# Moving one quad of exponentials in the last chunk of an attention block to VectorE, and new order constants for a kernel that plans its own instruction order

## The chip, the cores and the metric

One core of one Trainium2 chip. The metric is the device time of the one launch in microseconds; before the change the median of three runs is 809.28 us (809.02 to 810.05). Five engines work side by side, each through its own list of instructions in order: TensorE (PE, matmuls), ScalarE (ACT), VectorE (DVE), GpSimd (POOL) and SyncE (SP, which here only issues DMAs). They wait for each other through semaphores.

## The reference

An adaLN-conditioned transformer block over S = 2048 tokens of D = 640, with 32 heads of 20 and an MLP width of F = 1536, in bfloat16:

```
sa, ca, ga, sb, cb, gb = split(silu(c) @ w_mod, 6)
h = layernorm(x) * (1 + ca) + sa
q, k, v = split(h @ wqkv)
o = softmax(q k^T / sqrt(20)) v          # 32 heads, 2048 x 2048 scores each
x = x + ga * (o @ wo)
h = layernorm(x) * (1 + cb) + sb
x = x + gb * (((h @ w_gate) * (h @ w_up)) @ w_down)
```

Most of the element-wise work is the exponential: 32 x 2048 x 2048 of them.

## The kernel before

**Tiling.** The queries come in five chunks of 512, 512, 512, 256 and 256 (`CHUNKS`). The 32 heads are eight sets of four heads, one head for each group of 32 rows of the PE array. A pair of chunk and head set is an item, 40 in all, numbered 0 to 39 (`items`, the text calls them sets too; set 38 is the seventh head set of the last chunk). The work of an item is cut in units of 128 x 512 scores: 64 units in an item of the first three chunks, 32 in one of the last two.

**Two ways for an exponential.** A unit goes one of two ways.

- On ACT: two units at a time make a score round (L1492, the matmul of K and Q into one of two PSUM sets) and one ACTIVATE with Exp over 128 x 1024 (L1530, here called an exp). The results lie in PP, two buffers of four slots, so that eight exps may be outstanding; the product with V (L2179, from PP) frees a slot.
- On VectorE, by a piecewise approximation, four units at a time, a quad: each unit's score is evicted with an add and a max into int16 (L1554, to DB); then one operation over the whole quad masks out the mantissa (L1586, to DSS), one the exponent (L1594, to DSS), and mantissa times value is multiplied either on VectorE in one piece (L1591) or on GpSimd in four (L1646). Two terms come out of a quad, so that it costs PE twice the products with V (L2179, from DSS).

`QUADS[chunk][head set]` says how many quads an item has. All other units are ACT's.

**The end of an item.** When all its products with V are done, VectorE transposes the accumulator (L1724) and takes the reciprocal of the row sums (L1728), GpSimd multiplies (L1730, to OTn; VectorE in the last item), VectorE transposes back (L1738, to OcT), and four or five DMAs on SP's queue (L1751) write the rows to Ocp. Products of the next item use the same accumulator bank and start only after L1724. The last item is not written to Ocp: its OcT is used directly.

**The rest.** When a chunk is through, its suffix follows: the out projection (wo), the second layernorm, gate and up projections (weights loaded to stg and stx), and the down projection (wd). The suffix of a chunk is spread between the scores of the next one (L951, four narrow matmuls side by side); that of the last chunk is a tail behind everything (L947, wide matmuls). The projections of q, k and v lie mostly under the first chunk.

**What sets the order.** Nothing is ordered at run time. When it is built, the kernel runs a list scheduler (`Sched`, `pick_pe`): each task has a planned duration, and the order in which the scheduler starts them is written out as each engine's instruction list, with semaphore waits for the dependencies. Choices on PE (which comes next: a score round, products with V, a projection, or a filler matmul L2546 that only keeps PE active) hang on constants, and these may be overridden for each item in the table `STAGE`, taken over when the item's products with V begin (L2188, `stage`). The constants:

- `EAGER`, `D_LATE`, `D_RES`, `DL`: when the scores of a quad are due, how far ahead they may ride along with a score round, how late they force a round of their own, and when a PSUM bank is held back for them
- `PVMIN`, `PVMAX`, `PVCAP`, `PVTOL`: how many products with V are gathered before they are issued, and how far a batch may run past the time at which the next score round is ready
- `HOLD`, `X_LATE`: how long PE is left waiting for a score round that is nearly ready, and when a projection matmul is split into two halves to fit in front of one
- `FILL_MIN`, `FILL_Z`, `Z_LATE`: below which recent activity fillers are issued
- `XBACK`, `XDPRIO`, `TPRIO`: whether a quad's multiply may go to VectorE and with which priority against its other work
- `STEAL_GAP`: when ACT takes over a PSUM eviction

```
def stage(it):
    globals().update(base)
    globals().update(STAGE.get(it, {}))
...
t.cond = lambda c0=c0, st_=st_: st_["xby"] is None and c0() and xjob[0] >= XBACK
```

Of the kernel before, what the change touches and what calls it, by code (L numbers as in the profile page):

```python
# [29 lines left out]
STEAL_GAP = 200  # L30
# [299 lines left out]
def emit_program(nc, sched, nsem_dma=56):  # L330
# [97 lines left out]
    with nc.Block() as block:  # L428
# [20 lines left out]
        def _(e):  # L449
# [22 lines left out]
EAGER = 7  # L472
# [43 lines left out]
FILL_MIN = 4190.746  # L516
FILL_HARD = 0.0
FILL_Z, Z_LATE = 3300.0, 0.0
# [29 lines left out]
    8: {"PVCAP": 15, "PVMAX": 3, "Z_LATE": 19.94, "FILL_Z": 3656.07, "FILL_MIN": 4663.83, "TPRIO": 0.57, "X_LATE": -175.04, "EAGER": 16, "PVMIN": 1, "XBACK": 3, "STEAL_GAP": 194.45},  # L548
    9: {"X_LATE": -14.35, "PVCAP": 12, "XBACK": 0, "HOLD": 65, "PVMIN": 3, "D_LATE": 24, "PVMAX": 6, "D_RES": 23, "FILL_MIN": 4552.44, "XDPRIO": 1.63},
    10: {"PVMAX": 8, "X_LATE": -27.967, "EAGER": 5, "D_LATE": 15, "PVCAP": 8, "XBACK": 0, "HOLD": 155, "FILL_Z": 3693.44, "Z_LATE": -95.95, "PVMIN": 5, "XDPRIO": 1.25, "PVTOL": 199, "D_RES": 17},  # L550
    11: {"DL": 0.443, "X_LATE": 54.31, "FILL_MIN": 4086.76, "PVTOL": 270, "PVMAX": 6, "PVCAP": 14, "XBACK": 2, "D_LATE": 22, "Z_LATE": -74.79, "EAGER": 4},
    12: {"DL": 0.459, "FILL_MIN": 5116.53, "D_LATE": 11, "STEAL_GAP": 194.93, "X_LATE": -138.337, "HOLD": 125, "FILL_Z": 3256.59, "PVMIN": 1, "D_RES": 29},
    13: {"DL": 0.417, "D_RES": 4, "HOLD": 99, "PVMAX": 4, "TPRIO": 0.51, "PVMIN": 5, "STEAL_GAP": 145.61, "PVCAP": 13, "FILL_MIN": 4574.64, "FILL_Z": 2424.75, "PVTOL": 324, "Z_LATE": 38.05},
    14: {"D_LATE": 14, "D_RES": 16, "FILL_MIN": 4279.59, "EAGER": 11, "X_LATE": -150.94, "STEAL_GAP": 200, "PVTOL": 374, "FILL_Z": 3396.29, "HOLD": 50, "XDPRIO": 1.59, "PVMAX": 10, "TPRIO": 1.17, "PVCAP": 9},
    15: {"X_LATE": -189.21, "EAGER": 15, "Z_LATE": -100, "D_RES": 5, "HOLD": 65, "PVMAX": 4, "PVMIN": 4, "PVTOL": 199, "STEAL_GAP": 191.33, "FILL_MIN": 4305.09},
    16: {"D_RES": 67, "HOLD": 88, "PVCAP": 11, "PVMIN": 3, "PVTOL": 299, "STEAL_GAP": 83.35, "EAGER": 7, "Z_LATE": 121.81, "FILL_MIN": 4640.79, "FILL_Z": 2909.17, "D_LATE": 20, "X_LATE": 34.41},
    17: {"D_LATE": 23, "PVMAX": 10, "PVMIN": 5, "FILL_MIN": 4666.58, "EAGER": 4, "FILL_Z": 3806.89, "PVCAP": 9, "XBACK": 4, "Z_LATE": 10.27},
    18: {"FILL_MIN": 5006.36, "D_RES": 10, "X_LATE": 88.33, "FILL_Z": 2885.8, "HOLD": 80, "Z_LATE": -17.94, "PVTOL": 99, "XBACK": 0, "STEAL_GAP": 258.74, "EAGER": 5},
    19: {"DL": 0.471, "D_LATE": 16, "FILL_MIN": 3976.707, "HOLD": 140, "TPRIO": 1.09, "PVCAP": 15, "X_LATE": 3.27, "PVMAX": 10, "FILL_Z": 3225.84},
    20: {"DL": 0.391, "D_LATE": 14, "PVCAP": 13, "FILL_MIN": 5232.96, "FILL_Z": 3888.52, "HOLD": 110, "STEAL_GAP": 143.97, "X_LATE": 36.5, "XBACK": 0, "PVTOL": 174, "Z_LATE": 264.18, "EAGER": 5, "D_RES": 38},  # L560
    21: {"D_RES": 10, "PVCAP": 20, "HOLD": 111, "PVMAX": 3, "PVMIN": 2, "D_LATE": 19, "X_LATE": 10.44, "STEAL_GAP": 193.54, "FILL_MIN": 4451.89, "FILL_Z": 2458.3, "XBACK": 0, "Z_LATE": 146.94, "EAGER": 6},
    22: {"PVMAX": 4, "FILL_MIN": 2993.41, "D_RES": 17, "EAGER": 6, "D_LATE": 14, "PVCAP": 10, "PVTOL": 224, "STEAL_GAP": 173.23},
    23: {"PVTOL": 197, "PVMAX": 8, "D_RES": 23, "Z_LATE": -56.49, "STEAL_GAP": 273.34, "FILL_MIN": 5236.36, "EAGER": 7, "HOLD": 185, "FILL_Z": 4231.28, "D_LATE": 14, "XDPRIO": 1.93, "TPRIO": 1.16},
    24: {"DL": 0.464, "PVCAP": 13, "PVMAX": 9, "PVMIN": 2, "FILL_MIN": 4034.81, "EAGER": 7, "STEAL_GAP": 200, "X_LATE": 41.65, "HOLD": 125, "XDPRIO": 0.3, "D_LATE": 14},
    25: {"DL": 0.549, "STEAL_GAP": 200, "HOLD": 129, "X_LATE": 20.01, "D_RES": 13, "FILL_MIN": 3705.17, "PVCAP": 13, "D_LATE": 18, "PVMIN": 5, "Z_LATE": 116.92, "PVMAX": 9, "XBACK": 1},
    26: {"DL": 0.411, "D_RES": 15, "X_LATE": -208.68, "PVMAX": 9, "PVCAP": 14, "STEAL_GAP": 200, "FILL_MIN": 3859.63, "XBACK": 3, "EAGER": 8},
    27: {"DL": 0.473, "D_LATE": 6, "PVMAX": 6, "EAGER": 2, "D_RES": 75, "PVTOL": 249, "PVMIN": 2, "X_LATE": -93.66, "FILL_MIN": 4986.69},
    28: {"PVCAP": 13, "X_LATE": 94.44, "D_RES": 23, "HOLD": 80},
    29: {"PVCAP": 14, "PVMAX": 7, "D_RES": 46, "FILL_MIN": 3820.529, "HOLD": 65, "PVTOL": 299, "X_LATE": 14.16, "Z_LATE": -100},
    30: {"X_LATE": 10.24, "PVCAP": 19, "FILL_MIN": 3782.61, "D_LATE": 16, "EAGER": 9, "PVMAX": 4, "STEAL_GAP": 217.05, "PVTOL": 224, "XDPRIO": 1.57, "PVMIN": 1},  # L570
    31: {"D_RES": 19, "FILL_MIN": 4905.173, "D_LATE": 13, "PVMIN": 2, "X_LATE": 36.868, "HOLD": 155, "PVTOL": 274, "PVCAP": 13},
# [2050 lines left out]
```

## Time and profile before

| | |
|---|---|
| median of 3 runs | 809.28 us (809.02 to 810.05) |
| the profiled execution's own time | 809.42 us |
| its span in the profile | 807.6 us |
| busy: PE, ACT, DVE, POOL | 793.6, 764.0, 691.6, 364.6 us |
| exps (L1530) on ACT | 808, 743.8 us busy |
| quads on VectorE | 108 |
| mean granted PE clock | 1.00 |

The profile is one execution on the chip. A group of instructions is given as line, engine, operation, output<-input with its shapes, and count; then busy microseconds, the mean of one in ns, the idle time of the engine in front of them and what ended most of it. Matmuls are pipelined, so that the busy time of PE holds part of its waiting. ACT's operations overlap too: the busy time of a group is the union of its instructions, not their sum. In a timeline row stand start, duration, engine, line, operation and count, in brackets the idle time before it and what released it. The chain is followed back from the last instruction through what released each step. "issue" is time in which an engine waited for nothing that the profile shows.

### The profile page before, as it was taken

To read this page: it belongs to the slowest core of one execution; us is meant where nothing else is said; L and a number is where in the kernel's file an instruction comes from. 1 tells how busy PE (TensorE), PEld (TensorE's weight loads), DVE (VectorE), ACT (ScalarE), POOL (GpSimd) and SP (SyncE) were. 2 spreads that over 40 slices of the span, in tenths; PEclk is the share of its full clock that TensorE was granted. 3 is DMA by queue.
4 is the path that set the end of the run, shared out by engine and by line. 5 is a ranking of instruction groups with operands and counts; after the bars stand their busy time and mean duration, and the time that the engine had idled before them with its cause. 6 is when DMAs were issued, how large, how long until landed. Compare 5 with 4: busy or idle time off the path is not lost.

```text
span 807.6 us, 29760 instructions
## 1 busy us (share of the span) xinstructions
PE 793.6 (98%) x12789; PEld 307.5 (38%) x12789; DVE 691.6 (86%) x1275; ACT 764.0 (95%) x854; POOL 364.6 (45%) x370
## 2 busy tenths in 40 slices
PE   9999999999999999999999999999999999999998
PEld 4433333222233222333233333333245543544577
DVE  7979987999999899998998999999598874778873
ACT  7899999999999999999999999999999999999922
POOL 3303266465665452444456244334267552652710
PEclk9999999999999999999999999999999999999999
DMA  9624211114230235100401221001203363005010
GB/s 313 208 82 109 68 46 41 43 38 126 86 72 23 58 86 142 30 13 22 95 6 31 54 51 33 4 24 53 59 6 71 81 144 71 13 23 128 8 37 18
DMA packets 108577, 52.80 MB, mean 65 GB/s; under 512 B 76043, under 2 KB 108447, under 8 KB 108447
## 3 DMA queue, kind: packets, MB, share of 16 engines
q1 hardware_dynamic: 107519, 49.75, 23.4%
q8 instruction: 102, 1.67, 0.8%
q10 hardware_dynamic: 928, 1.15, 0.4%
q14 instruction: 28, 0.23, 0.1%
HBM read 39.88 MB, written 8.41 MB: 60 GB/s over the span
## 4 chain that ended last, share of the span: by engine, by line
PE 51%; ACT 38%; issue 6%; DVE 4%; DMA 1%; SPq 0%; ACTq 0%; DVEq 0%
ACT PP L1530 38%; PE ps_all L1492 16%; PE ps_all L951 16%; PE ps_all L2179 11%; PE ps_all L947 3%; DVE DB L1554 1%; PE ps_all L1211 1%; PE ps_all L2546 1%; DMA wm<-in_w_mod_dram 1%; PE ps_all L1147 1%; PE ps_all L1914 1%; DVE DSS L1586 1%; PE ps_all L1108 1%; DVE DSS L1594 0%; SPq L1751 0%
## 5 line engine op out<-in xcount | busy, mean ns | idle before, releaser
L1530 ACT ACTIVATE PP<-ps_all 128x1024 bf16<-128x1024 f32 x808 | 743.8, 1130 | 5.0 <-PE ps_all L1492 2.6
L1646 POOL TENSOR_TENSOR DSS<-DB,DSS 128x512 bf16<-128x512 bf16 x264 | 299.8, 1157 | 321.1 <-DVE DSS L1594 276.1
L1554 DVE TENSOR_SCALAR DB<-ps_all 128x512 int16<-128x512 f32 x432 | 287.9, 683 | 52.6 <-PE ps_all L1492 50.5
L1492 PE MATMUL ps_all<-QT,KT 32*128 32x512 bf16 (+1 forms) x2560 | 315.4, 340 | 7.2 <-ACT PP L1530 3.8
L1492 PEld LDWEIGHTS ps_all<-QT,KT 32*128 32x128 bf16 x2560 | 82.2, 91 | 260.6 <-ACT PP L1530 223.2
L2179 PE MATMUL ps_all<-PP,Vf 128*32 128x512 bf16 (+1 forms) x2032 | 158.2, 343 | 0.0
L951 PE MATMUL ps_all<-h2T,stg 128*32 128x512 bf16 (+2 forms) x1948 | 119.5, 326 | 0.1
L2179 PE MATMUL ps_all<-DSS,Vf 128*32 128x512 bf16 (+2 forms) x1056 | 85.0, 343 | 0.3 <-DVE DSS L1594 0.2
L1594 DVE TENSOR_SCALAR DSS<-DB 128x2048 int16<-128x2048 int16 x108 | 76.9, 712 | 0.1
L1586 DVE TENSOR_SCALAR DSS<-DB 128x2048 int16<-128x2048 int16 x108 | 76.0, 703 | 0.5
L2179 PEld LDWEIGHTS ps_all<-PP,Vf 128*32 128x32 bf16 x2032 | 45.1, 94 | 78.7 <-issue 72.4
L1730 POOL TENSOR_TENSOR OTn<-OT,invT 128x512 bf16<-128x512 f32 (+1 forms) x39 | 38.1, 977 | 52.4 <-DVE invT L1728 52.2
L951 PE MATMUL ps_all<-wd,hprod 128*32 128x320 bf16 (+1 forms) x1300 | 61.1, 286 | 0.2 <-DVE DB L1554 0.2
L951 PEld LDWEIGHTS ps_all<-h2T,stg 128*32 128x32 bf16 x1948 | 42.3, 95 | 35.9 <-issue 24.4
L1591 DVE TENSOR_TENSOR DSS<-DB,DSS 128x2048 bf16<-128x2048 bf16 x42 | 52.3, 1249 | 0.1
L951 PEld LDWEIGHTS ps_all<-wd,hprod 128*32 128x32 bf16 x1300 | 28.5, 96 | 21.1 <-issue 13.3
L2179 PEld LDWEIGHTS ps_all<-DSS,Vf 128*32 128x32 bf16 (+1 forms) x1056 | 27.0, 95 | 18.5 <-issue 8.9
L951 PE MATMUL ps_all<-wV,hT 128*32 128x320 bf16 (+1 forms) x696 | 32.5, 290 | 0.0
L1211 PE MATMUL ps_all<-hT,wq 128*32 128x512 bf16 x375 | 31.2, 383 | 0.2
L951 PE MATMUL ps_all<-wo,Ocp 128*32 128x320 bf16 (+1 forms) x660 | 30.3, 281 | 0.2
L2546 PE MATMUL ps_all<-ident 128*32 128x512 bf16 x344 | 30.0, 383 | 0.0
L1724 DVE STREAM_TRANSPOSE OT<-ps_all 128x512 f32<-128x512 f32 (+1 forms) x40 | 24.1, 602 | 6.0 <-PE ps_all L2179 5.8
(130 smaller groups left out, 528.6 us busy)
## 6 DMA issues: line engine op xcount, KB each, us to landing
stg<-in_B_w_gate_dram SPq DMA_DIRECT2D x44, 160.0 KB
stg<-in_B_w_up_dram SPq DMA_DIRECT2D x44, 160.0 KB, 3.1
QT<-q_rows SPq DMA_DIRECT2D x22, 128.0 KB, 2.4
KT<-k_rows SPq DMA_DIRECT2D x84, 32.0 KB, 2.6
wm<-in_w_mod_dram SPq DMA_DIRECT2D x3, 800.0 KB
x<-in_A_x_dram SPq DMA_DIRECT2D x7, 320.0 KB
xck<-in_A_x_dram SPq DMA_DIRECT2D x3, 640.0 KB, 4.5
wd<-in_B_w_down_dram SPq DMA_DIRECT2D x1, 1920.0 KB
```

Source lines behind the costliest of these rows:

```text
L951: return lambda e, b: e.matmul(ps[32 * x:32 * x + 32, b, c0 + o:c0 + o + w], lhs()[:, 32 * x:32 * x + 32], rhs() if w == n else rhs()[:, o ...
L1211: f = [lambda e, b_, k=k, x=x: e.matmul(ps[x:x + min(32, w - x), b_, :], wx[:, k, r0 + x:r0 + min(x + 32, w)], hT[tc][:, k, :], tile_posit ...
L1492: ems.append(lambda e, i=i, kt=kt: e.matmul(dstf()[:, i * u.n:(i + 1) * u.n], KT[32 * u.s:32 * u.s + 32, u.j, kt * 128:(kt + 1) * 128], QT ...
L1530: return e.activation(PPs[g % 2][:, cellp["p"], 0:nu * 512], ps[:, b0:b0 + nu, :].rearrange("p b c -> p (b c)"), AFT.Exp, scale=ESCALE)
L1554: return e.tensor_scalar(DBl[st_["slot"]][:, x * 512:(x + 1) * 512], bank(cell["b"]), EBIAS, 0.0, op0=ALU.add, op1=ALU.max)
L1586: return e.tensor_scalar(DSl[st_["ss"][0]][:, :], DBl[st_["slot"]][:, :], 0x7F, 0x3F00, op0=ALU.bitwise_and, op1=ALU.bitwise_or)
L1591: return e.tensor_tensor(d, DBl[st_["slot"]][:, :].bitcast(BF16), d, ALU.mult)
L1594: return e.tensor_scalar(DSl[st_["ss"][1]][:, :], DBl[st_["slot"]][:, :], 0x7F80, 2, op0=ALU.bitwise_and, op1=ALU.bitwise_or)
L1646: return e.tensor_tensor(d, DBl[st_["slot"]][:, x * w:x * w + w].bitcast(BF16), d, ALU.mult)
L1730: f3 = lambda e: e.tensor_tensor(OTn[:, 0:n].rearrange("p (b c r) -> p b r c", c=32, r=2), OT[:, 0:n].rearrange("p (b r c) -> p b r c", c= ...
L2179: ems.append(lambda e, i=i, kt=kt, stt=stt, stp=stp: e.matmul(ps[32 * s:32 * s + mc, BPV, 0:u.n], Vf[:, (kt * H + 4 * u.j + s) * VW:(kt * ...
L2546: task.emits = [lambda e, x=x: e.matmul(ps[32 * x:32 * x + 32, b_, :].rearrange("p (a b) -> p a b", a=4), ident[:, 32 * x:32 * x + 32], id ...
```

## The change

Two tables of constants change and no code. In the last chunk the first and third head sets (sets 32 and 34) get one quad more and the seventh (set 38) one less, 109 quads for 108. In `STAGE`, of the 40 entries those of sets 0 to 7, 14, 20, 23 and 38 stay, and the other 28, from set 8 on, get other values; which tasks exist besides the moved units does not hang on them, only their order, their engine where two are possible, and where a matmul is halved. Its core:

```
          (3, 5, 2, 4, 3, 4, 4, 4),
          (4, 2, 4, 4, 4, 4, 4, 4),
          (1, 2, 1, 2, 2, 1, 1, 2),
-         (0, 2, 1, 1, 3, 0, 3, 2))
+         (1, 2, 2, 1, 3, 0, 2, 2))
...
-    8: {..., "TPRIO": 0.57, "X_LATE": -175.04, "EAGER": 16, ..., "STEAL_GAP": 194.45},
-    9: {..., "D_RES": 23, "FILL_MIN": 4552.44, "XDPRIO": 1.63},
-    10: {"PVMAX": 8, ..., "HOLD": 155, ..., "PVMIN": 5, "XDPRIO": 1.25, "PVTOL": 199, "D_RES": 17},
+    8: {..., "TPRIO": 0.57, "EAGER": 16, ..., "STEAL_GAP": 194.45, "XDPRIO": 2.05},
+    9: {..., "D_RES": 23, "FILL_MIN": 4103.55, "XDPRIO": 1.63, "PVTOL": 224},
+    10: {"PVMAX": 9, ..., "HOLD": 110, ..., "PVMIN": 2, "XDPRIO": 1.25, "PVTOL": 199, "D_RES": 17},
...
-    34: {"X_LATE": 150, "D_LATE": 22, "FILL_MIN": 3900.9, ..., "PVMAX": 9, ..., "XBACK": 2, "Z_LATE": 90.81},
-    35: {..., "FILL_MIN": 2500, "STEAL_GAP": 179.748, ..., "HOLD": 121, ..., "EAGER": 12, "XBACK": 3, "XDPRIO": 1.7, ...},
-    36: {"DL": 0.524, ..., "X_LATE": 67.38, ..., "PVCAP": 15, ...},
-    37: {"D_LATE": 12, ..., "PVCAP": 13, ..., "XBACK": 1, "XDPRIO": 1.88, "HOLD": 65, ..., "FILL_Z": 4023.76},
+    34: {"X_LATE": 150, "D_LATE": 24, "FILL_MIN": 4158.98, ..., "PVMAX": 11, ..., "XBACK": 0, "Z_LATE": 90.81, "HOLD": 80},
+    35: {..., "FILL_MIN": 2704.26, "STEAL_GAP": 209.68, ..., "HOLD": 106, ..., "XBACK": 4, "XDPRIO": 0.37, ..., "EAGER": 8},
+    36: {"DL": 0.524, ..., "X_LATE": 8.69, ..., "PVCAP": 18, ...},
+    37: {"D_LATE": 14, ..., "PVCAP": 15, ..., "XDPRIO": 1.88, "HOLD": 35, ..., "FILL_Z": 3731.25, "PVMAX": 6, "EAGER": 9},
     38: {"D_RES": 60, "PVMAX": 7, "PVTOL": 375, "D_LATE": 14, "EAGER": 5, "TPRIO": 0.3, "FILL_MIN": 3948.58, "XBACK": 3, "X_LATE": 4.46},
-    39: {"FILL_MIN": 3089.11, ..., "EAGER": 8, "HOLD": 140, "XBACK": 3},
+    39: {"FILL_MIN": 3089.11, ..., "EAGER": 8, "XBACK": 3},
```

More of the change, by code (lines that the diff above doesn't have):

```diff
@@ new lines @@
+    9: {"X_LATE": -14.35, "PVCAP": 12, "XBACK": 0, "HOLD": 65, "PVMIN": 3, "D_LATE": 24, "PVMAX": 6, "D_RES": 23, "FILL_MIN": 4103.55, "XDPRIO": 1.63, "PVTOL": 224},
+    10: {"PVMAX": 9, "X_LATE": -27.967, "EAGER": 5, "D_LATE": 15, "PVCAP": 8, "XBACK": 0, "HOLD": 110, "FILL_Z": 3693.44, "Z_LATE": -95.95, "PVMIN": 2, "XDPRIO": 1.25, "PVTOL": 199, "D_RES": 17},
+    11: {"DL": 0.443, "X_LATE": 54.31, "FILL_MIN": 4086.76, "PVTOL": 270, "PVMAX": 6, "PVCAP": 14, "D_LATE": 22, "Z_LATE": -74.79, "EAGER": 4},
@@ new lines @@
+    12: {"DL": 0.459, "D_LATE": 11, "STEAL_GAP": 194.93, "X_LATE": -138.337, "HOLD": 125, "FILL_Z": 3256.59, "PVMIN": 1, "D_RES": 29},
+    13: {"DL": 0.417, "D_RES": 4, "HOLD": 99, "PVMAX": 4, "TPRIO": 0.51, "PVMIN": 5, "STEAL_GAP": 145.61, "PVCAP": 13, "FILL_MIN": 5235.75, "FILL_Z": 2424.75, "PVTOL": 324, "Z_LATE": -67.84, "XDPRIO": 1.14},
+    14: {"D_LATE": 14, "D_RES": 16, "FILL_MIN": 4279.59, "EAGER": 11, "X_LATE": -150.94, "STEAL_GAP": 200, "PVTOL": 374, "FILL_Z": 3396.29, "HOLD": 50, "XDPRIO": 1.59, "PVMAX": 10, "TPRIO": 1.17, "PVCAP": 9},
@@ new lines @@
+    15: {"X_LATE": -189.21, "EAGER": 15, "Z_LATE": -100, "D_RES": 5, "HOLD": 65, "PVMAX": 4, "PVMIN": 4, "PVTOL": 199, "STEAL_GAP": 191.33, "D_LATE": 14},
+    16: {"D_RES": 67, "HOLD": 88, "PVCAP": 11, "PVMIN": 3, "PVTOL": 299, "STEAL_GAP": 83.35, "EAGER": 7, "Z_LATE": 121.81, "FILL_MIN": 4640.79, "FILL_Z": 2909.17, "D_LATE": 20, "X_LATE": 34.41, "PVMAX": 8, "XBACK": 1},
+    17: {"D_LATE": 23, "PVMAX": 10, "PVMIN": 5, "FILL_MIN": 4231.45, "EAGER": 4, "FILL_Z": 3806.89, "PVCAP": 9, "XBACK": 4, "Z_LATE": 101.76, "TPRIO": 1.29, "HOLD": 80},
@@ L562 @@
-    22: {"PVMAX": 4, "FILL_MIN": 2993.41, "D_RES": 17, "EAGER": 6, "D_LATE": 14, "PVCAP": 10, "PVTOL": 224, "STEAL_GAP": 173.23},
+    21: {"D_RES": 10, "PVCAP": 20, "HOLD": 111, "PVMAX": 3, "PVMIN": 2, "X_LATE": 32.77, "STEAL_GAP": 193.54, "FILL_MIN": 4085.58, "FILL_Z": 2458.3, "XBACK": 0, "Z_LATE": 146.94, "EAGER": 8, "TPRIO": 0.3, "XDPRIO": 1.17, "PVTOL": 224},
+    22: {"PVMAX": 4, "FILL_MIN": 2500, "D_RES": 17, "EAGER": 6, "D_LATE": 14, "PVCAP": 10, "PVTOL": 224, "STEAL_GAP": 189.38, "FILL_Z": 4191.54, "HOLD": 200, "X_LATE": -70.46, "PVMIN": 4},
@@ new lines @@
+    25: {"DL": 0.549, "STEAL_GAP": 200, "HOLD": 129, "X_LATE": 20.01, "D_RES": 13, "FILL_MIN": 3705.17, "PVCAP": 13, "D_LATE": 18, "PVMIN": 5, "Z_LATE": 116.92, "PVMAX": 6, "XBACK": 1, "EAGER": 9, "TPRIO": 0.94, "FILL_Z": 3555.45},
+    26: {"DL": 0.411, "D_RES": 15, "X_LATE": -208.68, "PVMAX": 9, "PVCAP": 14, "STEAL_GAP": 200, "FILL_MIN": 4203.59, "XBACK": 3, "EAGER": 8},
+    27: {"DL": 0.473, "D_LATE": 6, "PVMAX": 6, "EAGER": 1, "D_RES": 72, "PVTOL": 249, "PVMIN": 1, "X_LATE": -183.07, "FILL_MIN": 4986.69},
@@ new lines @@
+    28: {"PVCAP": 13, "X_LATE": 111.56, "D_RES": 23, "HOLD": 80},
+    29: {"PVCAP": 14, "PVMAX": 7, "D_RES": 46, "FILL_MIN": 3820.529, "HOLD": 65, "PVTOL": 299, "X_LATE": 68.11, "Z_LATE": -100},
+    30: {"X_LATE": 10.24, "PVCAP": 19, "FILL_MIN": 3782.61, "D_LATE": 16, "EAGER": 6, "PVMAX": 4, "STEAL_GAP": 217.05, "PVTOL": 224, "XDPRIO": 1.57, "PVMIN": 1, "Z_LATE": -100},
+    31: {"D_RES": 19, "FILL_MIN": 4905.173, "D_LATE": 13, "PVMIN": 1, "X_LATE": 36.868, "HOLD": 155, "PVTOL": 274, "PVCAP": 13, "EAGER": 9, "FILL_Z": 3497.58},
@@ new lines @@
+    32: {"PVMIN": 1, "D_RES": 78, "XDPRIO": 0.559, "XBACK": 0, "X_LATE": 64.4, "FILL_Z": 2584.21, "EAGER": 3, "HOLD": 80},
+    33: {"DL": 0.442, "STEAL_GAP": 199.702, "D_LATE": 18, "PVCAP": 15, "PVMAX": 3, "PVTOL": 353, "D_RES": 17, "PVMIN": 2, "HOLD": 70, "XDPRIO": 1.72, "EAGER": 3, "Z_LATE": 136.87, "FILL_MIN": 4090.6, "XBACK": 0, "TPRIO": 0.45, "X_LATE": 17.09, "FILL_Z": 2760.65},
+    34: {"X_LATE": 150, "D_LATE": 24, "FILL_MIN": 4158.98, "EAGER": 5, "PVTOL": 324, "XDPRIO": 1.43, "PVMAX": 11, "FILL_Z": 2145.7, "TPRIO": 0.5, "XBACK": 0, "Z_LATE": 90.81, "HOLD": 80},
@@ new lines @@
+    35: {"PVMIN": 5, "PVMAX": 8, "FILL_MIN": 2704.26, "STEAL_GAP": 209.68, "X_LATE": -108.93, "HOLD": 106, "D_LATE": 8, "XBACK": 4, "XDPRIO": 0.37, "FILL_Z": 2961.24, "EAGER": 8},
+    36: {"DL": 0.524, "PVMIN": 2, "D_RES": 10, "X_LATE": 8.69, "PVMAX": 10, "HOLD": 108, "PVCAP": 18, "STEAL_GAP": 251.53, "PVTOL": 174, "FILL_MIN": 4037.09},
+    37: {"D_LATE": 14, "PVTOL": 179, "PVCAP": 15, "X_LATE": -66.154, "TPRIO": 0.3, "XDPRIO": 1.88, "HOLD": 35, "STEAL_GAP": 181.37, "PVMIN": 5, "FILL_MIN": 4146.64, "FILL_Z": 3731.25, "PVMAX": 6, "EAGER": 9},
```

32 lines of the change are left out of this document (5 added, 27 removed).

## The prediction

> **What bounds the kernel now.** I read the page first: busy time and the chain (parts 1, 2, 4), then the groups (part 5).
>
> ```profile
> span 807.6 us, 29760 instructions
> PE 793.6 (98%) x12789; PEld 307.5 (38%) x12789; DVE 691.6 (86%) x1275; ACT 764.0 (95%) x854; POOL 364.6 (45%) x370
> ...
> PE 51%; ACT 38%; issue 6%; DVE 4%; DMA 1%; SPq 0%; ACTq 0%; DVEq 0%
> ...
> L1530 ACT ACTIVATE PP<-ps_all 128x1024 bf16<-128x1024 f32 x808 | 743.8, 1130 | 5.0 <-PE ps_all L1492 2.6
> L1646 POOL TENSOR_TENSOR DSS<-DB,DSS 128x512 bf16<-128x512 bf16 x264 | 299.8, 1157 | 321.1 <-DVE DSS L1594 276.1
> L1554 DVE TENSOR_SCALAR DB<-ps_all 128x512 int16<-128x512 f32 x432 | 287.9, 683 | 52.6 <-PE ps_all L1492 50.5
> ...
> L1594 DVE TENSOR_SCALAR DSS<-DB 128x2048 int16<-128x2048 int16 x108 | 76.9, 712 | 0.1
> L1586 DVE TENSOR_SCALAR DSS<-DB 128x2048 int16<-128x2048 int16 x108 | 76.0, 703 | 0.5
> ...
> L1591 DVE TENSOR_TENSOR DSS<-DB,DSS 128x2048 bf16<-128x2048 bf16 x42 | 52.3, 1249 | 0.1
> ...
> L2546 PE MATMUL ps_all<-ident 128*32 128x512 bf16 x344 | 30.0, 383 | 0.0
> ```
>
> ScalarE (ACT) runs 808 exps and sits idle in front of them for 5.0 us in all: from the first to the last exp the kernel is paced by ACT. The exps overlap (1130 ns each, yet 743.8 us for 808), so what one costs is their pitch. Three views of L1530 (the timeline over 214 to 576 us and over 672 to 770, and the source line in 192 to 213) give it:
>
> ```profile
> 212.88 364.39 ACT L1530 ACTIVATE PP<-ps_all 128x1024 bf16<-128x1024 f32 x396
> ...
> 671.24 93.35 ACT L1530 ACTIVATE PP<-ps_all 128x1024 bf16<-128x1024 f32 x101
> 765.90 3.77 ACT L1530 ACTIVATE PP<-ps_all 128x1024 bf16<-128x1024 f32 x4 [1.31 <-PE ps_all L2179]
> ```
>
> ```profile
> L1530 ACT ACTIVATE PP<-ps_all x25: 1051/1210/1346, 191.2 to 212.9; 128x1024 bf16<-128x1024 f32 x25
> ```
>
> 364.39 less one exp's 1.13, over 395, is 0.920 us; the last row has 24 pitches in 21.7 us, 0.904 us, which I take as the undisturbed pitch. The difference, 0.016 us, is what the order of the work costs today: 9.4 us over the 590 exps of sets 8 to 38 (sets numbered 0 to 39 over the five chunks). The third row is one real hole, 1.31 us, four exps from the end, and it waits for L2179, the product with V. The last exp ends at 769.67; behind it comes a tail that PE and its waits set. It is read from the timeline over 758 to 808 us (start, duration, engine, line, what it waited for) and from the chain over 757 to 808 us:
>
> ```profile
> 764.00 0.12 PEld L1492 LDWEIGHTS ps_all<-QT,KT 32*128 32x128 bf16 x6 [0.21 <-issue]
> ...
> 764.82 0.45 DVE L1724 STREAM_TRANSPOSE OT<-ps_all 128x256 f32<-128x256 f32 x1
> ...
> 768.02 0.39 PE L1492 MATMUL ps_all<-QT,KT 32*128 32x256 bf16 x4
> ...
> 768.93 4.06 SPq L1751 DMA_DIRECT2D Ocp<-OcT  x5
> ...
> 772.67 0.39 PE L2179 MATMUL ps_all<-DSS,Vf 128*32 128x256 bf16 x8
> ...
> 774.14 1.26 PE L947 MATMUL ps_all<-wo,Ocp 128*128 128x320 bf16 x8 [1.07 <-DMA Ocp<-OcT]
> ```
>
> ```profile
> 764.41 0.34 PE ps_all L2179 x8
> ...
> 765.08 0.32 PE ps_all L1492 x4
> ...
> 765.62 1.09 PE ps_all L2179 x40
> ```
>
> The seventh head set of the last chunk (set 38) is transposed at 764.82, written out by five DMAs from 768.93, and they let the out projection (L947) start at 774.14, when PE had been out of work since 773.06 (772.67 + 0.39). From there to the end of the span are 33.5 us.
>
> **The change, part by part.** Counted in the instruction orders of both builds, up to score matmul 563 (set 8) they are the same; the exps' own order on ACT is the same throughout, only two shorter.
>
> *Two exps fewer.* A quad is four units, an exp two. One quad more net (109 for 108) takes 808 exps to 806: 2 x 0.920 = -1.84 us. The quad adds on VectorE four L1554 and one each of L1586 and L1594, 4 x 0.683 + 0.703 + 0.712 = 4.15 us, one L1591 more (43 for 42, 1.25), and on PE eight products with V more (16 more from DSS, 8 fewer from PP): 8 x 0.027 = 0.2 us. VectorE is hidden if its quads come in time (rival C); PE's 0.2 us lies beside 16 fillers fewer (L2546, 328 for 344).
>
> *The hole at the end.* PP holds eight exps. Counting score rounds less the exps that L2179 has consumed, the order before lets 8 pile up at the end: set 39's products may not start until set 38 is finished, and set 38, with three quads in ten exps, finishes only four score rounds before the last. That is the L2179 x40 at 765.62, with ACT empty. In the changed order set 38 has two quads and twelve exps, and its last product stands seven score rounds before the last; at most five exps are outstanding. The hole goes: -1.31 us. What is late next is PE: those seven intervals hold 6.4 us of PE work by the rows above, and seven exps take 7 x 0.92 = 6.4 us. So they just fit; bounds 0 and -1.4.
>
> *The tail.* From the last exp's score round (768.02) to L947 is 6.12 us before, 1.07 of it PE idle for the DMA. After: PE's work behind the last score round is 140 projection and 24 V matmuls, for 112 and 40. At 1.09/40 = 0.027 us each that is 164 x 0.027 = 4.47, with the score round's 0.32 and a change of tile shape of 0.12 (0.34 for x8 less 8 x 0.027, in the chain) 4.92 us. The same count for before, with a second score piece of 0.32, gives 152 x 0.027 + 0.64 + 0.24 = 5.03, and the rows give 773.06 - 768.02 = 5.04. Does the DMA come in time? From set 38's transpose to L947 were 774.14 - 764.82 = 9.32 us. After, that transpose follows the score round seven before the last by 0.82 us (764.00 to 764.82), so it is 7 x 0.92 - 0.82 = 5.6 us ahead of the last round; + 9.32 lands 3.7 us behind it, 4.9 if VectorE's L1591, which now lies between, costs its 1.25 us. PE is there at 4.92. So L947 starts 4.92 us behind the last round: -1.20 us (bounds 0, if the chain of OTn, OcT and five DMAs slips by 1.2 us, and -1.4). The rest is the same instructions: four projection matmuls move past the transposes, and ACT takes three of the five h2T evictions instead of two, under 92 matmuls that run meanwhile: nothing.
>
> *The order constants.* Stages 8 to 39 get other times for filling, balancing and attaching. The set of tasks stays, halved matmuls shift (160-wide pieces of the down projection 296 to 360). Bounds: they could win back the 9.4 us of pitch above 0.904, or lose as much again. Pricing every stretch between two score rounds (score 0.32, 0.027 a tile matmul, 0.12 a change), PE's mean from set 8 on is 0.888 us before and 0.890 after, and the stretches above 1.06 us are 36 for 22. Fourteen more, each some 0.18 us over the exp pitch, are 2.6 us if none is absorbed; the scores run a round ahead, so that most is. Before, the same stretches summed to 17 us above 0.905, of which no more than 9.4 reached ACT, hardly in the same places. I take +0.3 us, close to the lower end, because the means agree.
>
> Sum: -1.84 - 1.31 - 1.20 + 0.3 = -4.05 us. The profiled execution took 809.42 us (1.8 outside its span), 0.14 above the median of 809.28; so 805.4 in its terms and **805.2 us** beside the median.
>
> **A rule that speaks against it.** VectorE's two whole-quad operations do not always take their median; the source views of both:
>
> ```profile
> L1586 DVE TENSOR_SCALAR DSS<-DB x108: 629/683/1537, 42.8 to 769.8; 128x2048 int16<-128x2048 int16 x108
> L1594 DVE TENSOR_SCALAR DSS<-DB x108: 651/686/1534, 43.4 to 770.5; 128x2048 int16<-128x2048 int16 x108
> ```
>
> The maximum is 0.85 us above the median. The Trainium skill ("SBUF — State Buffer", SBUF: two separate sides) says that VectorE in its two-port modes and GpSimd take a shared port pair as an exclusive lock and that the loser blocks for the whole instruction. By that rule, a quad more means two more chances to stand behind a GpSimd piece, 2 x 1.157 us of VectorE at worst; the trace agrees in kind (the stretched maxima), but its medians say that it is rare. No number of the forecast hangs on it.
>
> **The rivals.**
> *A: the tail does not shorten.* Set 38's chain slips (GpSimd does its OTn between multiply pieces of 1157 ns) and L947 again waits for the DMA. For it: that chain had a wait of 1.07 us before. Against: 1 us of room by the count. 806.4 us; with the hole kept too, 807.7.
> *B: the new order gives the gain back.* The 14 heavier stretches each cost their 0.18 us and more, +2.6 to +6 us: 807.7 to 810.9. For it: PE at 98% with stretches near the exp pitch. Against: the same mean and an exp buffer that mostly holds two or three.
> *C, slower: late quads in sets 24 to 31.* Counted by median durations between the sets' transposes, VectorE's load there goes up by 5.8 us (87.9 to 93.7, beside 104 exps, 95.7 us); the multiplies move to it from GpSimd. If its operations also stretch, quads finish late, PP fills as it did at 765 and each set ends in a hole of 1.31 us. From five of the eight sets on it is slower than before: 805.2 + 5 x 1.31 = 811.8; all eight, 815.7. Against it, the count is too high, since it mixes shapes: in the windows view VectorE is busy for 75.88 us of that stretch, and 20 are free:
>
> ```profile
> 576.00:672.00 96.00, 75.88 (x155) 1.00 0.30 68
> ```
>
> That the change does not do what it says is out: 806 exps and 436 L1554 are in the built order.
>
> **How the numbers follow.** Forecast 805.2 (range of its own 803.5 to 806.6): 0.60. A 0.10. B 0.13. C 0.10. Better still, order constants that win pitch back, below 803.5: 0.07. The range 803.4 to 809.0 takes in the forecast, A, and the nearer half of B, and leaves out C, the rest of B and the best cases, some 0.2. A measurement tells 0.2%, 1.6 us, from no change: faster is below 807.7 (forecast, A, the better case: 0.77), same to 810.9 (B: 0.13), slower above (C: 0.10).
>
> **What would show it.** 806 exps at a pitch of 0.92 us; no ACT idle of a microsecond for L2179 near the end; L947 with no wait for the DMA, some 4.9 us behind the last score round and 33.5 us before the end. A pitch above 0.927 between 214 and 670 us would show B; ACT waiting for L2179 in 576 to 672, C; L947 waiting on Ocp, A.

## The result and the profile after

The changed kernel takes 805.69 us (median of 5 runs, 805.64 to 806.13) beside 809.14 us for the kernel before (5 runs, 809.02 to 810.05): ratio 0.9956, 95% interval 0.9942 to 0.9971. Its profiled execution took 805.69 us; 803.8 of it are the span.

The page of the changed kernel, first the span, the busy times and the chain's shares, then three groups (line, engine, operation, count, busy us, mean ns, idle us in front):

```profile
span 803.8 us, 29783 instructions
PE 790.9 (98%) x12801; PEld 306.6 (38%) x12801; DVE 693.3 (86%) x1283; ACT 762.1 (95%) x851; POOL 364.1 (45%) x370
...
PE 61%; ACT 31%; DVE 4%; issue 3%; DMA 1%; ACTq 0%; DVEq 0%
...
L1530 ACT ACTIVATE PP<-ps_all 128x1024 bf16<-128x1024 f32 x806 | 742.2, 1136 | 3.9 <-PE ps_all L1492 3.0
...
L1554 DVE TENSOR_SCALAR DB<-ps_all 128x512 int16<-128x512 f32 x436 | 290.3, 683 | 57.5 <-PE ps_all L1492 54.5
...
L2546 PE MATMUL ps_all<-ident 128*32 128x512 bf16 x328 | 29.0, 383 | 0.0
```

There are two exps fewer, four L1554 more and 16 fillers fewer, as the built order said. The idle time in front of the exps falls from 5.0 to 3.9 us. The page no longer names L2179 among the releasers: of 2.1 us of waits for it before, one of 0.8 us is left, in front of set 8. SP's queue has left the chain.

The exps of the changed kernel in the timeline, over 214 to 576 us and then over 670 to 770 us (start, duration, count, in brackets the idle time in front):

```profile
212.78 123.37 ACT L1530 ACTIVATE PP<-ps_all 128x1024 bf16<-128x1024 f32 x134
336.54 240.70 ACT L1530 ACTIVATE PP<-ps_all 128x1024 bf16<-128x1024 f32 x262 [0.39 <-PE ps_all L1492]
...
668.98 97.98 ACT L1530 ACTIVATE PP<-ps_all 128x1024 bf16<-128x1024 f32 x106
```

The last row runs to the last exp without a break: the hole four exps from the end is gone. A small one has come at 336.54, in set 13.

The tail, from the timeline of all engines over 752 to 776 us: set 38's transpose, SP's row of the DMAs to Ocp (set 38's stand at its end), the last score round, and the out projection:

```profile
759.87 0.44 DVE L1724 STREAM_TRANSPOSE OT<-ps_all 128x256 f32<-128x256 f32 x1
...
752.00 16.53 SPq L1751 DMA_DIRECT2D Ocp<-OcT  x7
...
765.43 0.39 PE L1492 MATMUL ps_all<-QT,KT 32*128 32x256 bf16 x4
...
770.34 1.12 PE L947 MATMUL ps_all<-wo,Ocp 128*128 128x320 bf16 x7
```

L947 has no wait in brackets, and it starts 770.34 - 765.43 = 4.91 us behind the last score round. "The last score round" means the round of the last exp throughout; in the kernel before it starts at 768.02.

**Where the time came from.** Five stretches add up to the difference of the spans (807.62 and 803.83 to two digits). The starts of sets 8 and 39 are those of their first exp.

| stretch | before | after | difference |
|---|---|---|---|
| start to set 8 | 213.79 | 213.70 | -0.09 |
| set 8 to set 39 | 543.12 | 541.97 | -1.15 |
| set 39 to the last score round | 11.11 | 9.76 | -1.35 |
| last score round to L947 | 6.12 | 4.91 | -1.21 |
| L947 to the end | 33.48 | 33.49 | +0.01 |
| sum | 807.62 | 803.83 | -3.79 |

Two exps at the 0.92 us of the prediction are -1.84 us, so that the second row holds +0.69 us for the order. One profile stands for each kernel here, and stretches scatter by a few tenths: up to set 8 the built orders of all the kernels below are the same, and that stretch takes 213.70 to 214.10 us in them.

### The profile page after: what moved, and what is told of

Read it like the earlier page. It is cut to its first block, busy times and chain, and to the rows that moved or that the text cites. A ratio compares the mean times of both kernels' runs of the same rounds, so it can differ in the third digit from the quotient of the medians.

```text
span 803.8 us, 29783 instructions
## 1 busy us (share of the span) xinstructions
PE 790.9 (98%) x12801; PEld 306.6 (38%) x12801; DVE 693.3 (86%) x1283; ACT 762.1 (95%) x851; POOL 364.1 (45%) x370
## 3 DMA queue, kind: packets, MB, share of 16 engines
q10 hardware_dynamic: 928, 1.15, 0.4%
## 4 chain that ended last, share of the span: by engine, by line
PE 61%; ACT 31%; DVE 4%; issue 3%; DMA 1%; ACTq 0%; DVEq 0%
ACT PP L1530 30%; PE ps_all L1492 20%; PE ps_all L951 20%; PE ps_all L2179 14%; PE ps_all L947 3%; DVE DB L1554 1%; PE ps_all L2546 1%; PE ps_all L1211 1%; DMA wm<-in_w_mod_dram 1%; PE ps_all L1914 1%; PE ps_all L1147 1%; PE ps_all L1108 1%; DVE wd L1475 1%; DVE DSS L1586 0%; DVE DSS L1594 0%
## 5 line engine op out<-in xcount | busy, mean ns | idle before, releaser
L1530 ACT ACTIVATE PP<-ps_all 128x1024 bf16<-128x1024 f32 x806 | 742.2, 1136 | 3.9 <-PE ps_all L1492 3.0
L1646 POOL TENSOR_TENSOR DSS<-DB,DSS 128x512 bf16<-128x512 bf16 x264 | 300.3, 1158 | 321.7 <-DVE DSS L1594 275.1
L1554 DVE TENSOR_SCALAR DB<-ps_all 128x512 int16<-128x512 f32 x436 | 290.3, 683 | 57.5 <-PE ps_all L1492 54.5
L2179 PE MATMUL ps_all<-PP,Vf 128*32 128x512 bf16 (+1 forms) x2024 | 159.1, 344 | 0.0
L951 PE MATMUL ps_all<-h2T,stg 128*32 128x512 bf16 (+2 forms) x1912 | 117.7, 329 | 0.0
L2179 PE MATMUL ps_all<-DSS,Vf 128*32 128x512 bf16 (+3 forms) x1072 | 85.1, 343 | 0.3 <-DVE DSS L1594 0.2
L1594 DVE TENSOR_SCALAR DSS<-DB 128x2048 int16<-128x2048 int16 x109 | 77.5, 711 | 1.3 <-PE ps_all L2179 1.2
L1586 DVE TENSOR_SCALAR DSS<-DB 128x2048 int16<-128x2048 int16 x109 | 74.9, 687 | 0.3
L2179 PEld LDWEIGHTS ps_all<-PP,Vf 128*32 128x32 bf16 x2024 | 44.6, 94 | 80.3 <-issue 75.3
L1730 POOL TENSOR_TENSOR OTn<-OT,invT 128x512 bf16<-128x512 f32 (+1 forms) x39 | 37.2, 953 | 53.5 <-DVE invT L1728 53.5
L951 PE MATMUL ps_all<-wd,hprod 128*32 128x320 bf16 (+1 forms) x1332 | 60.1, 283 | 0.2 <-DVE xck L2060 0.2
L951 PEld LDWEIGHTS ps_all<-h2T,stg 128*32 128x32 bf16 x1912 | 41.4, 95 | 31.1 <-issue 22.2
L951 PEld LDWEIGHTS ps_all<-wd,hprod 128*32 128x32 bf16 x1332 | 29.3, 96 | 19.3 <-issue 11.5
L2179 PEld LDWEIGHTS ps_all<-DSS,Vf 128*32 128x32 bf16 (+1 forms) x1072 | 26.6, 95 | 20.8 <-issue 11.9
L951 PE MATMUL ps_all<-wV,hT 128*32 128x320 bf16 (+1 forms) x696 | 32.5, 290 | 0.0
L951 PE MATMUL ps_all<-wo,Ocp 128*32 128x320 bf16 (+1 forms) x660 | 29.9, 281 | 0.1
L1724 DVE STREAM_TRANSPOSE OT<-ps_all 128x512 f32<-128x512 f32 (+1 forms) x40 | 24.1, 603 | 5.3 <-PE ps_all L2179 5.3
```

Source lines behind the costliest of these rows:

```text
L951: return lambda e, b: e.matmul(ps[32 * x:32 * x + 32, b, c0 + o:c0 + o + w], lhs()[:, 32 * x:32 * x + 32], rhs() if w == n else rhs()[:, o ...
L1530: return e.activation(PPs[g % 2][:, cellp["p"], 0:nu * 512], ps[:, b0:b0 + nu, :].rearrange("p b c -> p (b c)"), AFT.Exp, scale=ESCALE)
L1554: return e.tensor_scalar(DBl[st_["slot"]][:, x * 512:(x + 1) * 512], bank(cell["b"]), EBIAS, 0.0, op0=ALU.add, op1=ALU.max)
L1586: return e.tensor_scalar(DSl[st_["ss"][0]][:, :], DBl[st_["slot"]][:, :], 0x7F, 0x3F00, op0=ALU.bitwise_and, op1=ALU.bitwise_or)
L1594: return e.tensor_scalar(DSl[st_["ss"][1]][:, :], DBl[st_["slot"]][:, :], 0x7F80, 2, op0=ALU.bitwise_and, op1=ALU.bitwise_or)
L1646: return e.tensor_tensor(d, DBl[st_["slot"]][:, x * w:x * w + w].bitcast(BF16), d, ALU.mult)
```

## The experiments

Each text names the theory held when it was written (T) and its rivals. Times are medians of 5 to 11 runs, with the ratio to the kernel before on the same chip and its 95% interval. "The tail" is the stretch from the last score round to the end of the span.

### The quads alone, the constants alone

q_only has the new `QUADS` and all the old constants, s_only the reverse.

```
 q_only:  (0, 2, 1, 1, 3, 0, 3, 2)  ->  (1, 2, 2, 1, 3, 0, 2, 2)      STAGE as before
 s_only:  QUADS as before,  STAGE[8..39] as after
```

> The new quad counts with all order constants as before. Theory T (the terms of the prediction, plus PE's work behind the last score round as counted in the built order): two exps fewer -1.84 us, no more than four exps outstanding at the end so that the hole of 1.31 us goes, the wait for set 38's DMAs (1.07 us) goes because its last product stands seven score rounds before the last, but 56 more gate/up matmuls are left behind the last score round than in the changed kernel: +1.8 us. Sum -2.6 us against before, 806.5 us. Rival K (the gain lies in the order constants, the quads alone give their exps): -1.8 us, 807.3 us, with the hole still there. Rival Q (the gain lies in the quads alone): as the changed kernel, 805.7 us.

> The new order constants with the quad counts as before. T: 808 exps; set 38 has three quads again and finishes only two score rounds before the last, PP fills, so the hole of about 1.3 us stays; its DMAs land some 8 us behind the last score round instead of 6.1; 2.2 us less PE work lies behind that round; the stall of 0.7 us from the early constants comes on top. About 809.8 us, no gain. Rival K: the constants carry the gain, some 807 us. Rival Q: 809.1 us.

Measured: q_only 808.75 us, 0.9992 (0.9983 to 1.0); s_only 813.38 us, 1.0051 (1.0037 to 1.0065). Neither part alone gives a gain that can be told from none, and the constants alone lose. The effects do not add up: -0.65 and +3.98 us against the median of before on the same chip (809.4), -3.45 together. T, at 806.5 and 809.8 us, missed both, by 2.25 and 3.6 us, and both rivals missed too.

What s_only loses is seen at once. Its exps in the timeline over 740 to 771 us (the window cuts off the last two exps):

```profile
740.52 25.06 ACT L1530 ACTIVATE PP<-ps_all 128x1024 bf16<-128x1024 f32 x27 [0.30 <-PE ps_all L1492]
769.99 1.94 ACT L1530 ACTIVATE PP<-ps_all 128x1024 bf16<-128x1024 f32 x2 [4.40 <-PE ps_all L2179]
```

It is the hole of the kernel before, in the same place and for the same releaser, but 4.40 us wide for 1.31: with three quads in set 38, the new order makes it worse.

q_only has no such hole, its two exps are gone, and L947 waits for no DMA. Its last score round (765.74) is within 0.3 us of the changed kernel's (765.43). Yet it ends 3.1 us later. The last rows of PE in the chain of q_only, and below them those of the changed kernel and of the kernel before (start, duration, what):

```profile
777.07 1.25 PE ps_all L951 x32
778.32 0.67 PE ps_all L1914 x10
778.99 5.55 PE ps_all L951 x160
784.53 19.77 PE ps_all L947 x180
```

```profile
770.41 3.23 PE ps_all L947 x23
...
774.13 3.37 PE ps_all L951 x96
777.51 0.67 PE ps_all L1914 x10
778.17 3.24 PE ps_all L951 x92
781.41 19.77 PE ps_all L947 x180
```

```profile
777.93 3.51 PE ps_all L951 x100
781.44 0.67 PE ps_all L1914 x10
782.10 3.10 PE ps_all L951 x88
785.20 19.77 PE ps_all L947 x180
```

The last row, the last chunk's own gate, up and down projections, is the same in all three and sets the end. L1914 are the transposes of the layernorm in front of it. Between the two PE works off the L951 that is left of the chunk before: 160 matmuls in q_only, 92 in the changed kernel, 88 in the kernel before. In the built order q_only has 196 gate and up matmuls (L951 on h2Tt) behind its last score round; the changed kernel has 140 and the kernel before 112.

Beside the kernel before, q_only is 0.29 us later at set 8 (scatter, the orders are the same), 1.29 us shorter over sets 8 to 38, 1.28 shorter from there to the last round, and 1.61 longer in the tail. Of sets 8 to 38 T had two exps, -1.84, so that the order cost 0.55 us with the old constants too. In the tail T lacked 0.88 us of new idle time, in the table below.

### The third quad of set 38 by itself

q38to32 moves one quad from set 38 to set 32 and keeps 108; q32add gives set 32 one more and leaves set 38 its three. Both have the old constants.

```
 before   (0, 2, 1, 1, 3, 0, 3, 2)
 q38to32  (1, 2, 1, 1, 3, 0, 2, 2)
 q32add   (1, 2, 1, 1, 3, 0, 3, 2)
```

> One quad moved from set 38 to set 32, 108 in all, constants as before. T: 808 exps, at most a few exps outstanding at the end, so hole gone (-1.4 us) and DMA wait gone (-1.3 us), 1.3 us more PE work behind the last score round: -1.4 us, 807.7 us. Rival E (the gain follows the number of exps alone): 809.1 us. If only the work in front of the out projection counts, and not all of PE's work to the end, 806.4 us.

> One quad more in set 32, none taken from set 38, 109 in all, constants as before. T: exps -1.84 us; set 38 finishes three score rounds before the last as before, so that its DMAs again hold the out projection (nothing gained there, although 1.9 us less PE work is left); seven exps outstanding, one short of filling PP, so the hole goes in part (0 to -1.4 us): -1.84 to -3.2 us, 806 to 807.3 us, with L947 waiting for the DMA. Rival E (exps alone): 807.3 us. Rival (PE's work behind the last score round alone): 804 us.

Measured: q38to32 809.28 us, 0.9999 (0.999 to 1.0008); q32add 811.05 us, 1.0019 (1.0011 to 1.0028). T missed both, by 1.6 us and by some 4 us. Rival E had the number of q38to32 (809.1), but by luck: the hole and the wait for the DMA are gone, and other time takes their place. The exps of q38to32 and then of q32add in the timeline over 740 to 771 us:

```profile
739.27 29.72 ACT L1530 ACTIVATE PP<-ps_all 128x1024 bf16<-128x1024 f32 x32
```

```profile
739.88 23.58 ACT L1530 ACTIVATE PP<-ps_all 128x1024 bf16<-128x1024 f32 x25
768.43 2.85 ACT L1530 ACTIVATE PP<-ps_all 128x1024 bf16<-128x1024 f32 x3 [4.98 <-PE ps_all L2179]
```

So the hole hangs on the third quad of set 38: it is there in the kernel before, s_only, q32add and early (below), and in none of the nine kernels with two quads there. The built orders agree. Count as outstanding at a score round the rounds in front of it less the exps whose products with V all stand in front of it: with three quads this reaches nine at the third round from the end, in all four kernels, and with two quads no more than five in set 39. T of q32add had seven.

How wide the hole is does not follow from that count. Three rows of the chain through the hole of q32add, where ACT is empty from 763.45 to 768.43:

```profile
765.35 1.71 PE ps_all L951 x56
...
767.28 0.87 PE ps_all L951 x32
768.15 1.10 PE ps_all L2179 x40
```

The chain is VectorE's from 762.48 to 765.31 (evictions and the two operations over a quad); then PE works off 88 gate and up matmuls in front of the 40 products that free PP. In s_only 128 stand in the same place, in the kernel before 16. They are missing behind the last round, where q32add has 44 and s_only 40 for 112, so that a part of the tail's work is done here, while ACT stands empty.

But taking the hole away is worth nothing by itself. q38to32 also starts its out projection early, 1.74 us behind the start of its last exp; its chain over the last 40 us shows where that goes:

```profile
769.67 3.31 PE ps_all L947 x23
...
773.55 3.72 PE ps_all L951 x132
...
778.64 6.70 PE ps_all L951 x192
785.35 19.77 PE ps_all L947 x180
```

L947 x23 starts 4.5 us sooner than in the kernel before and the last group 0.15 us later: all 192 down projection matmuls now stand behind the transposes.

### Parts of the constants

early is the kernel before with the new constants of sets 8 to 23; mid and late are the changed kernel's quads with the new constants of sets 24 to 39 and of 32 to 39 only.

```
 early:  QUADS as before;  STAGE[8..23]  as after, [24..39] as before
 mid:    QUADS as after;   STAGE[24..39] as after, [8..23]  as before
 late:   QUADS as after;   STAGE[32..39] as after, [8..31]  as before
```

> The kernel before with the new order constants of sets 8 to 23 alone. The instructions behind the last score round are counted the same as before, and so is PP's filling at the end. T: the pitch of the exps rises in sets 8 to 23, in set 13 above all (a hole near 335 us), +0.7 us: 809.8 us. Rival: the early constants are what gains, 807 us or less.

> The new quad counts, new order constants for sets 24 to 39, those of sets 8 to 23 as before. Its built order leaves 3.5 us more PE work behind the last score round than the changed kernel. T: exps -1.84, hole -1.4, DMA wait -1.3, tail work +3.6 us: -0.9 us, 808.2 us. If the tail hangs on the work in front of the out projection alone (as in the changed kernel): 805.1 us.

> The new quad counts, new order constants for sets 32 to 39 alone, those of sets 8 to 31 as before. T with the whole of PE's work to the end as the measure of the tail: exps -1.84, hole -1.4, DMA wait -1.3, tail work +1.6 us: -2.9 us, 806.2 us. If only the work in front of the out projection sets the tail (1.8 us less than in the changed kernel): 804.8 us. If the early constants cost the changed kernel 0.7 us and nothing else differs: 805.0 us.

Measured: early 809.15 us, 0.9997 (0.9988 to 1.0006); mid 809.67 us, 1.0003 (0.9994 to 1.0012); late 807.6 us, 0.998 (0.9971 to 0.9989). The loss of 0.7 us that T expected of early did not come: its small hole at 336.54 is there, but the time cannot be told from the kernel before. late is the telling one. Its last exp starts at 765.45, before that of the changed kernel (765.89), its out projection at 768.22 for 770.34, and it still ends 1.8 us later. Its chain:

```profile
775.86 0.73 PE ps_all L1914 x10
776.59 6.63 PE ps_all L951 x192
783.23 19.77 PE ps_all L947 x180
```

Again all 192 are behind the transposes. The tails side by side, for kernels without a hole at the end and the kernel before; the PE work is counted in the built orders and priced as in the prediction (0.32 a score round, 0.027 a narrow matmul, a wide one by its columns), idle is PE's from the timeline's brackets:

| | gate/up L951 behind the last round | PE work | PE idle on a wait | last round to the end | rest |
|---|---|---|---|---|---|
| before | 112 | 34.68 | 1.07 (Ocp) | 39.60 | 3.85 |
| after | 140 | 34.74 | 0 | 38.40 | 3.66 |
| q_only | 196 | 36.49 | 0.88 | 41.21 | 3.84 |
| q38to32 | 184 | 35.94 | 0.71 | 40.46 | 3.81 |
| late | 188 | 36.27 | 0.61 | 40.63 | 3.75 |
| mid | 268 | 38.24 | 0.20 | 42.23 | 3.79 |

The rest is nearly the same in all, so that the tail is the work left behind the last score round plus PE's waits. Where L947 starts within it makes no difference. (The work of q_only and late holds four fillers, 0.2 us.) T priced the work left for the tail, but not PE's new idle time there nor the order under the exps, and so came out too low by 2.25 us for q_only, 1.6 for q38to32, 1.4 for late and 1.5 for mid. The new idle times are waits for VectorE's layernorm and product work (xn2c, sd, hprodt).

### One set's constants put back

Four kernels are the changed one with a single entry of `STAGE` put back: a13 (set 13), back17, back18 and back35.

```
 a13:     STAGE[13] as before, all else as after
 back17:  STAGE[17]   "     back18:  STAGE[18]   "     back35:  STAGE[35]   "
```

> The changed kernel with set 13's order constants from before. The work behind the last score round is counted the same. T: the hole near 335 us in set 13 goes, and with it up to 1.0 us; other sets are ordered anew, so 0.4 of it may come back: 804.7 to 805.3 us. Rival: order constants in one set cost nothing that lasts, 805.7 us.

> The changed kernel with the constants of set 18 alone put back; quads, exps (806) and the PE work behind the last score round (34.74 us) are those of the changed kernel. Counting score rounds less exps consumed by products with V in its built order, PP is six or more full at 20 score rounds behind set 8, against 1 in the changed kernel and 6 in the one with set 13 put back. T: such fillings are what ACT pays for when VectorE is late (5 us in the run with set 13 put back), so that this one loses as well, 807 to 811 us, with ACT idle for L2179 in sets 18 to 31 and the same distance from the last exp to the end (37.94 us). R: the fill count of a built order tells nothing; only exps and the work left for the tail count, 805.7 us.

> The changed kernel with the constants of set 17 alone put back: 806 exps, 34.74 us of PE work behind the last score round, PP six or more full only once, all as in the changed kernel. T: no hole, 805.7 us (805.2 to 806.5). The rival, that any reordering which the constants were not chosen together for loses some microseconds, as with set 13: 808 us or more.

> The changed kernel with the constants of set 35 alone put back: 806 exps, 8 projection matmuls fewer behind the last score round (34.52 us of PE work for 34.74), PP six or more full only once. T: the work left for the tail decides, 805.5 us, 0.2 us less than the changed kernel, from the last exp to the end 37.7. The rival: what leaves the tail costs ACT its pitch in sets 35 to 39, no gain or a loss, 805.7 to 807.

Measured: a13 810.76 us, 1.0016 (1.0007 to 1.0025); back18 808.47 us, 0.999 (0.9982 to 0.9999); back17 805.76 us, 0.9957 (0.9944 to 0.9971); back35 806.25 us, 0.9964 (0.9951 to 0.9976). T was right for back18 and back17 and wrong for a13, which was to gain 0.4 to 1.0 us and lost 5: the small hole in set 13 is still there (0.38 us), and new ones have come. The tails of a13, back18 and back17 are the changed kernel's (38.40 or 38.41 us): the work behind their last score round is the same. What differs is exps: the time above a pitch of 0.905 us in sets 8 to 31 is 8.47 us in the changed kernel, 13.52 in a13, 11.27 in back18, 8.77 in back17.

The exps of a13 over 400 to 576 us, and the chain of waits through its large hole, over 419 to 430 us:

```profile
399.11 26.87 ACT L1530 ACTIVATE PP<-ps_all 128x1024 bf16<-128x1024 f32 x29
428.55 47.77 ACT L1530 ACTIVATE PP<-ps_all 128x1024 bf16<-128x1024 f32 x52 [2.57 <-PE ps_all L2179]
```

```profile
422.22 0.35 DVE xn L1900
422.57 0.40 DVE st L1892
422.97 0.39 DVE xck L1878
...
427.43 0.64 DVE OT L1724
428.06 0.04 issue
428.11 1.33 PE ps_all L2179 x15
429.44 0.04 issue
429.47 1.03 ACT PP L1530
```

From 419.9 to 428.06 the chain is VectorE alone, more than half of it the suffix (the add behind the out projection, L1878, and the layernorm, L1892, L1894 and L1900). The transpose of set 16 (L1724) stands behind that in VectorE's list, the next set's products with V wait for it, PP is full, and ACT stands still. This is the mechanism of rival C in another place and with another cause.

back18, over 214 to 600 us, has four smaller holes in sets 20 to 23, one of them for L2179:

```profile
496.33 22.14 ACT L1530 ACTIVATE PP<-ps_all 128x1024 bf16<-128x1024 f32 x24 [0.34 <-PE ps_all L1492]
518.93 22.13 ACT L1530 ACTIVATE PP<-ps_all 128x1024 bf16<-128x1024 f32 x24 [0.47 <-PE ps_all L1492]
542.15 22.11 ACT L1530 ACTIVATE PP<-ps_all 128x1024 bf16<-128x1024 f32 x24 [1.08 <-PE ps_all L2179]
564.41 35.93 ACT L1530 ACTIVATE PP<-ps_all 128x1024 bf16<-128x1024 f32 x39 [0.16 <-PE ps_all L1492]
```

The 20 and 6 of back18's expectation do not come out of the built orders. By the count of outstanding exps given above, seven or more are reached behind set 8 at 7 rounds of back18 and 8 of a13, for 1 in the changed kernel, back17 and back35. One of these, in set 10, is common to all and has no hole behind it. The others lie in sets 17, 19 and 21 of a13 and 20 to 23 of back18, the sets of nearly all their new holes, so that the count shows where ACT is likely to wait. It does not tell how long: at equal peaks the hole at the end was 1.31, 4.40 and 4.98 us wide. back17 loses nothing. back35's tail is 0.21 us shorter (38.19), as its 8 projection matmuls fewer say, but sets 32 to 39 give back 0.73 us of pitch (2.59 above 0.905 for 1.86): its rival was right. None of the kernels run beats the changed one.

## Why the prediction was right, point by point

- **Two exps fewer, -1.84 us.** In agreement, to a few tenths. q_only and q38to32 have the same constants, no hole at the end, and differ by one quad: their last exps start at 766.32 and 767.87, 1.55 us apart, with 0.29 us more time above the pitch of 0.905 in sets 8 to 39 of q_only. What two exps are worth and what the order costs cannot be told apart more closely than that.
- **The hole at the end, -1.31 us.** Right; -1.35 in the table. The cause, three quads in set 38, is shown by s_only and q32add (hole kept, and wider) against nine kernels with two quads there and none. The prediction's eight outstanding exps are nine by the count above; the five are right. That a hole can be 1.31 or 4.98 us wide with the same quad count was not foreseen.
- **The tail, -1.20 us.** The size was right, -1.21 to L947, and -1.20 to the end. But the step "the rest is the same instructions" was a finding about this pair of orders, and not a consequence of the quads. The two have the same work behind the last round, 34.68 and 34.74 us, so that the whole gain is the 1.07 us wait for the DMA and 0.1 beside it. With the old constants q_only frees L947 of the same wait and has 1.75 us more work left, and 0.88 of new idle time. late and q38to32 show that an earlier L947 is worth nothing by itself.
- **The order constants, +0.3 us.** Measured +0.69: 0.60 in sets 8 to 31 and 0.09 in sets 32 to 38. The sign was right and the size too small; with it the sum is -3.7 instead of -4.05. The remaining part of the miss is the base: the profiled execution of before is 0.28 us above its median, that of after lies on it. Of the 0.60, 0.4 to 0.6 are the constants': sets 8 to 31 take 458.35 to 458.54 us in the five kernels with the old ones there (before, q_only, q38to32, q32add, late) and 458.95 or 458.96 in the changed kernel, s_only and back35. Most of it lies in sets 24 to 31. In sets 32 to 38 the order is that of quads and constants together, and there the constants help: 83.36 us in q_only, 83.02 in the changed kernel. What the step did not see is that they also decide how much projection work is left for the tail. With the quads as they are the last score round comes at 765.74 with the old constants and at 765.43 with the new, so that under the exps they cost next to nothing; in the tail they are worth 2.8 us, 41.21 for 38.40, which is why the quads alone gave only -0.65.
- **Rival A** (L947 waits on Ocp again) did not come. Set 38's transpose is 5.56 us ahead of the last round, 5.6 in the prediction.
- **Rival B** (the order gives the gain back) came at a quarter of its lower end in the changed kernel. (That end, +2.6 us in place of +0.3, works out at 807.5 us and not at the 807.7 of the prediction.) a13 and back18, one entry apart from it, do lose 5.1 and 2.8 us to the order of the work, so that it was a real danger, decided by the whole set of constants.
- **Rival C** (VectorE late in sets 24 to 31) did not come as a loss of its own. The windows view of the changed kernel for the stretch of the prediction, with VectorE's busy time, its instructions in brackets:

```profile
576.00:672.00 96.00, 79.68 (x161) 1.00 0.31 70
```

  3.8 us more than before (75.88), 16 us still free, no exp there waits for L2179, and the time above the pitch in sets 24 to 31 grows by 0.5 us only.
- **The rule on the shared port pair** (the Trainium skill, "SBUF — State Buffer", SBUF: two separate sides) may have reached an exp once, at the small hole in set 13. VectorE and then GpSimd of the changed kernel, from the timeline over 330 to 337.5 us:

```profile
333.25 0.66 DVE L1586 TENSOR_SCALAR DSS<-DB 128x2048 int16<-128x2048 int16 x1
333.82 1.54 DVE L1594 TENSOR_SCALAR DSS<-DB 128x2048 int16<-128x2048 int16 x1
335.28 1.27 DVE L1554 TENSOR_SCALAR DB<-ps_all 128x512 int16<-128x512 f32 x2
```

```profile
333.42 1.40 POOL L1730 TENSOR_TENSOR OTn<-OT,invT 128x512 bf16<-128x512 f32 x1 [7.94 <-DVE invT L1728]
```

  L1594 is 0.85 us longer than its median and ends 0.54 us after L1730 does (335.36 and 334.82). The next score round waits for VectorE, and the exp has its 0.39 us. That VectorE stands behind GpSimd here is shown by all the traces together. In the 13 kernels L1586 and L1594 run 2826 times. In 2524 of these no GpSimd operation runs beside them, and none takes over 0.70 us. 126 take over 0.8 us: in each, a GpSimd multiply (L1646 or L1730) is running when it starts, and each ends 0.54 to 0.55 us after that one does, however long the two overlap. Beside 60 of them L1730 starts later, and none is stretched. So VectorE begins when GpSimd is through, which agrees with the rule; that a port is the reason, no run can tell. The prediction's two more chances did not show: 9 instructions are over 0.8 us for 10 in the kernel before. early and a13 have the same stretched L1594 and the same hole, mid and late neither; the sets that these kernels have in common point to the new constants of sets 8 to 12.

**Still open:** which of the constants of sets 8 to 39 bring the projection work under the exps. late (sets 32 to 39) leaves 188 gate and up matmuls, mid (24 to 39) 268, all together 140. No run singles one out.

## What to carry to other kernels

Where PE is 98% busy and another engine paces the main stretch, price a tail by the work left behind the last paced instruction and the waits in it, counted in the built order, and not by when the first step of the tail starts: that start moved by 4.5 us in one of these kernels and the end by nothing. A change of the split and the order planned for it are one change, to be tried together: they gave -0.65 and +3.98 us apart and -3.45 together, and one entry of forty put back cost between nothing and 5 us. Where a built order leaves the buffer between two engines nearly full can be counted before a run; that count told where ACT stood still, but not for how long.

## What the runs showed of the hardware

- An exp over 128 x 1024 takes 1136 ns in the changed kernel's page and follows the one before after 0.90 to 0.92 us: 742.2 us of busy time for 806, 0.921 each. The two figures differ by 0.2 us, and only the second prices an exp that is added or taken away.
- VectorE's whole-quad operations L1586 and L1594 take 0.68 us. When a GpSimd multiply was already running they ended 0.54 to 0.55 us after it and took up to 1.54 us; when it started after them they were not stretched. Over 0.8 us were 9 of 218 in the changed kernel, and one of these stands in the chain through the only hole behind set 8, 0.39 us of ACT's time.
